# Pooled attention with a routed feed-forward network: row sums by a GpSimd add and block-wise VectorE sums, the ranking in smaller pieces, the first loads in halves

## The chip, the cores and the metric

The kernel runs on one core of one Trainium2 chip. The metric is device time in microseconds (us) of one execution. Three runs of the kernel before took 950.93, 951.79 and 951.79 us, median 951.79. A profiled execution took 951.33 us; its trace spans 949.5 us, and the remaining 1.8 us lie around the span. All numbers "from the trace" are of that execution.

A core has five engines that run side by side, each with its own queue, in order: TensorE (PE in the profile, with PEld for its weight loads), VectorE (DVE), ScalarE (ACT), GpSimd (POOL) and SyncE (SP), which here only issues transfers. An instruction at the head of a queue that waits for another engine holds up everything behind it in its own queue.

## The reference

```python
def _attn_ref(q, k, v):                      # B=8, H=8, S=1152, D=64, fp32
    q_pool = q.reshape(B, H, S // 2, 2, D).mean(axis=3)
    scores = np.matmul(q_pool, k.transpose(0, 1, 3, 2)) / np.sqrt(D)
    attn = np.exp(scores - np.max(scores, axis=-1, keepdims=True))
    attn = attn / (np.sum(attn, axis=-1, keepdims=True) + 1e-09)
    return np.matmul(attn, v)                # (8, 8, 576, 64)

def _moe_ref(x, w_gate, w1, w2, capacity):   # x (8, 576, 512), F=1024, capacity=128
    scores = np.einsum('bsd,d->bs', x, w_gate)
    out = x.copy()
    for b in range(B):
        top_idx = np.argpartition(-scores[b], capacity)[:capacity]
        xe = x[b, top_idx]
        ye = np.maximum(xe @ w1, 0.0) @ w2
        g = 1.0 / (1.0 + np.exp(-scores[b, top_idx]))
        out[b, top_idx] = x[b, top_idx] + g[:, None] * ye
    return out
```

Queries are pooled in twos, attention is computed for 64 heads, and the heads of a batch make a row of 512 per token. In each of the 8 batches the 128 tokens with the highest gate score go through a two-layer feed-forward network (FFN).

## The kernel before

**Pairs, halves, steps.** Two heads of a batch are a *pair* (32 pairs, 4 to a batch). A pair's 576 queries are two *halves* of 288 (s = 0, 1), and the 1152 keys of a half are taken in three *groups* (g = 0, 1, 2) of three 128-key chunks. One group of one half is a *step*. A pair has 6 steps, i = 0 to 5, the kernel 192, and `run` writes the work out step by step; nothing reorders it. In each step, `scores` (L710, L717) multiplies keys with queries, two heads beside each other in the array, and ScalarE takes the exponent into a tile `p` of 128 x 3 x 2 x 288; keys lie on partitions, so a row sum runs over partitions and chunks. `weighted` (L727) then multiplies the `p` of the step before with the values and accumulates `av` over the three groups. So TensorE's queue is: scores of this step, `av` of the last step, and what the step has besides.

**The row sums.** `added` adds the three `p` tiles of a half on VectorE: `acc` = p0 + p1 (L745, 1728 columns), `acc` += p2 (L745), then the three chunks of `acc` into `sum` (L755, L756, 576 columns each). In the first step of the next half, `drained` (L760) transposes `av` out of PSUM in 32 x 32 blocks into `avb`. In the second step of the next half, `normalized` lets TensorE sum `sum` over the partitions with a matrix of ones (L770, two products of 288 columns, one for each head); VectorE transposes the result out of PSUM (`smb`, L778), adds 1e-9, takes the reciprocal and multiplies `avb` with it into `x` (L786). After a pair's second half, `finished` (i = 1 of the next pair) stores `x` in DRAM by four transfers (`xs`, L798), multiplies it with the gate weights on GpSimd (`prod`, L803) and sums that on VectorE (`part`, L809).

**The FFN.** `routed` is a generator that `run` advances once in a step, but not in the steps that call `normalized`. It begins at i = 1 of the batch's following pair and does in turn: the gate scores of a batch into one row (`line`, `diag`, two products L842), the same as columns (`columns`, five small products), the rank of each of five token tiles (L880, L889, L899, two tiles between two yields), the choice of 128 tokens (`pick`, `rank`, products L926, `index`), the gather of their rows (L938, GpSimd's queue), its transposition (L953), two layers (L965 twice 32 product records, L977 16), and the scatter (L992). For the last batch all of it stands at the end, behind `outside`, which checks the row sums' bounds.

**Tiles that are reused.** All small products share the pool `ps_ms` with one PSUM buffer (`misc`), `av` has one (`ps_av`), the scores three (`ps_sc`), `p` has five SBUF buffers.

**Loads.** `load_pair` issues, all on SP, four quarters of keys (`kb`) and of queries (`qb`), 144 KB each in pieces of 128 bytes, and two transfers of values. `prepare_pair` pools the queries on GpSimd (`qp`, L692) and transposes keys and queries block-wise on VectorE (`kT` L697, `qT` L698). Pair n+1 is loaded at i = 0 of pair n and prepared at i = 3. SP runs ahead of the other engines: it is held by the four `xs` transfers, which wait for `x`, and by transfers under way, of which the program allows eight before it waits for the oldest. The FFN weights (4.2 MB) are loaded behind pair 1.

## Time and profile before

| what | value |
|---|---|
| median of three runs | 951.79 us |
| profiled execution, its span | 951.33 us, 949.5 us |
| busy: TensorE, VectorE, ScalarE, GpSimd | 844.1, 629.0, 359.5, 109.4 us |
| first scores start | 14.36 us |
| scores of pair 1 start | 34.23 us |
| last `av` starts, last instruction's issue starts | 892.5, 944.1 us |
| a batch in the steady state (588.9 to 702.1) | 113.2 us |
| granted TensorE clock, mean | 0.946 |

Busy time is summed over the whole span, and each engine's share is an average. A line of a group of instructions names the source line, the engine, the operation, output and input tiles and their shapes, the number of instructions, busy time and the mean duration of one. A line of waits says which engine's instruction sat idle for which other, how long in total, how often, and the longest. A line of the timeline has the start, the duration, the engine, the line, and in brackets the idle time before it and who ended it. A matrix product in fp32 shows as two records.

### The profile page before, as it was taken

The numbers are of one execution on the slowest core, as the hardware profiler recorded it, in microseconds if no ns is written. First come the engines' busy times: TensorE is split into PE (matmuls) and PEld (weight loads), VectorE is DVE, ScalarE is ACT, GpSimd is POOL, SyncE is SP. The second block draws the span as 40 slices with busy tenths as digits, with TensorE's granted clock in tenths as the row PEclk, the third lists the DMA queues.
The fourth block names the chain that finished last, engine by engine and source line by source line (L and its number), as shares of the span: only waits on it lengthen the run. The fifth ranks groups of instructions, "written<-read, shape, count | busy, mean of one in ns | idle before, by whom it ended". The sixth has DMA issues, their size and how long they took to land.

```text
span 949.5 us, 14253 instructions
## 1 busy us (share of the span) xinstructions
PE 844.1 (89%) x5695; PEld 500.2 (53%) x5695; DVE 629.0 (66%) x1069; ACT 359.5 (38%) x625; POOL 109.4 (12%) x91
## 2 busy tenths in 40 slices
PE   4999888998899988999879989799889998889736
PEld 2555545654456554565446545465455654556324
DVE  2888777566875678746787376865777567874540
ACT  2544443434343344325424344343443334433200
POOL 1111111011110111102011111011111011110100
PEclk9999998999999999999999999899998999989958
DMA  9987774766834676545767437557464667810120
GB/s 134 249 135 103 125 105 60 83 99 109 104 56 61 94 138 88 76 61 74 125 88 99 60 77 117 82 88 99 89 97 64 76 99 118 108 24 7 25 67 14
DMA packets 453419, 84.97 MB, mean 89 GB/s; under 512 B 450528, under 2 KB 450528, under 8 KB 453088
## 3 DMA queue, kind: packets, MB, share of 16 engines
q1 hardware_dynamic: 452064, 79.79, 57.5%
q0 software_dynamic: 1280, 4.20, 1.6%
q8 instruction: 46, 0.75, 0.4%
q14 instruction: 29, 0.24, 0.1%
HBM read 72.42 MB, written 20.97 MB: 98 GB/s over the span
## 4 chain that ended last, share of the span: by engine, by line
issue 39%; PE 27%; DVE 18%; SPq 5%; POOL 5%; DMA 4%; ACT 2%; POOLq 0%; DVEq 0%
PE sc L710 9%; PE av L727 8%; DVE acc L745 6%; PE ps L965 6%; DMA qb<-in_q_dram 3%; POOL qp L692 3%; SPq L675 2%; SPq L798 2%; DVE cmp L889 2%; PE ps L977 1%; SPq L678 1%; ACT p L717 1%; DVE sum L755 1%; POOL prod L803 1%; PE ps L926 1%
## 5 line engine op out<-in xcount | busy, mean ns | idle before, releaser
L717 ACT ACTIVATE p<-sc 128x576 f32<-128x576 f32 x576 | 336.1, 651 | 408.3 <-PE sc L710 389.6
L710 PE MATMUL sc<-qT,kT 64*128 64x288 f32 x2304 | 352.3, 438 | 9.9 <-DVE qT L698 9.9
L727 PE MATMUL av<-p,v_sb 128*64 128x288 f32 x2304 | 332.2, 425 | 22.7 <-DVE avb L760 22.7
L710 PEld LDWEIGHTS sc<-qT,kT 64*128 64x128 f32 x2304 | 221.0, 195 | 124.3 <-issue 71.8
L727 PEld LDWEIGHTS av<-p,v_sb 128*64 128x64 f32 x2304 | 152.3, 140 | 181.7 <-issue 77.1
L745 DVE TENSOR_TENSOR acc<-p 128x1728 f32<-128x1728 f32 x64 | 124.6, 1947 | 115.4 <-ACT p L717 115.1
L745 DVE TENSOR_TENSOR acc<-acc,p 128x1728 f32<-128x1728 f32 x64 | 137.0, 2141 | 10.0 <-ACT p L717 9.5
L803 POOL TENSOR_TENSOR prod<-x,w_gate 128x576 f32<-128x576 f32 x32 | 44.9, 1403 | 568.9 <-DVE x L786 568.9
L760 DVE STREAM_TRANSPOSE avb<-av 128x288 f32<-128x288 f32 x64 | 30.6, 478 | 60.0 <-PE av L727 60.0
L965 PE MATMUL ps<-xeT,w 128*128 128x128 f32 x512 | 63.4, 284 | 1.4 <-ACT hT L972 0.7
L965 PEld LDWEIGHTS ps<-xeT,w 128*128 128x128 f32 x512 | 60.3, 197 | 8.1 <-issue 5.3
L977 PE MATMUL ps<-w,hT 128*128 128x512 f32 x128 | 57.1, 599 | 0.7 <-ACT hT L972 0.7
L809 DVE TENSOR_REDUCE part<-prod 128x18 f32<-128x576 f32 x32 | 24.1, 753 | 48.7 <-POOL prod L803 48.7
L755 DVE TENSOR_TENSOR sum<-acc 128x576 f32<-128x576 f32 x64 | 49.6, 775 | 2.2
L756 DVE TENSOR_TENSOR sum<-sum,acc 128x576 f32<-128x576 f32 x64 | 49.6, 775 | 2.2
L692 POOL TENSOR_TENSOR qp<-qb 128x576 f32<-128x576 f32 x32 | 45.9, 1435 | 22.8 <-DMA qb<-in_q_dram 22.6
L697 DVE STREAM_TRANSPOSE kT<-kb 128x1152 f32<-128x1152 f32 x32 | 43.0, 1345 | 6.2 <-DMA kb<-in_k_dram 6.2
L770 PE MATMUL ps<-sum,ones 128*64 128x288 f32 x256 | 42.7, 413 | 1.5 <-DVE sum L756 1.5
L977 PEld LDWEIGHTS ps<-w,hT 128*128 128x128 f32 x128 | 23.7, 190 | 30.7 <-issue 29.8
L926 PE MATMUL ps<-meta,pick 128*128 128x3 f32 (+1 forms) x80 | 15.3, 310 | 27.3 <-DVE pick L916 27.3
L972 ACT ACTIVATE hT<-ps 128x512 f32<-128x512 f32 x16 | 9.6, 597 | 73.8 <-PE ps L965 73.8
L984 DVE SCALAR_TENSOR_TENSOR xe<-ps,own_gate,xe 128x512 f32<-128x512 f32 x8 | 6.0, 751 | 41.9 <-PE ps L977 41.9
(64 smaller groups left out, 307.6 us busy)
## 6 DMA issues: line engine op xcount, KB each, us to landing
kb<-in_k_dram SPq DMA_DIRECT2D x128, 144.0 KB, 4.6
qb<-in_q_dram SPq DMA_DIRECT2D x128, 144.0 KB, 4.8
v_sb<-in_v_dram SPq DMA_DIRECT2D x64, 288.0 KB, 5.3
xs<-x SPq DMA_DIRECT2D x128, 72.0 KB, 2.3
out_dram<-xs SPq DMA_DIRECT2D x8, 1152.0 KB, 5.7
w<-in_moe_w_dram SPq DMA_DIRECT2D x2, 2048.0 KB, 11.1
xe<-xs,index POOLq DMA_INDIRECT x8, 3.5
out_dram<-xe,index POOLq DMA_INDIRECT x8, 4.4
```

Source lines behind the costliest of these rows:

```text
L692: nc.gpsimd.tensor_tensor(out=qp[:, :, :], in0=pair["q"][:, :, 0, :], in1=pair["q"][:, :, 1, :], op=ALU.add)
L697: nc.vector.transpose(pair["kT"][:, :], pair["k"].rearrange("p n d -> p (n d)"))
L710: nc.tensor.matmul(sc[:, j, 0:n], lhsT=pair["kT"][rows, c * P : (c + 1) * P], rhs=pair["qT"][rows, qs], start=True, stop=True,)
L717: nc.scalar.activation(grp["p"][:, u, :, :], sc[:, :, 0:n], AF.Exp, scale=self.scale)
L727: nc.tensor.matmul(self.av[j * self.D : (j + 1) * self.D, 0:n], lhsT=grp["pair"]["v"][:, j, c, :], rhs=grp["p"][:, u, j, :], start=(c == 0 ...
L745: nc.vector.tensor_tensor(out=acc[:, :, :], in0=first[:, :, :], in1=grp["p"].rearrange("p u j n -> p u (j n)"), op=ALU.add,)
L755: nc.vector.tensor_tensor(out=to, in0=acc[:, 0, :], in1=acc[:, 1, :], op=ALU.add)
L756: nc.vector.tensor_tensor(out=to, in0=to, in1=acc[:, 2, :], op=ALU.add)
L770: nc.tensor.matmul(ps[j * self.D : (j + 1) * self.D, 0:n], lhsT=self.ones[:, 0 : self.D], rhs=half["sum"][:, j, :], start=True, stop=True,)
L803: nc.gpsimd.tensor_tensor(out=prod[:, :, :], in0=x[:, hp, :, :], in1=self.w_gate[:, hp : hp + 1, :].broadcast_to([P, self.QB, BLK]), op=AL ...
L965: nc.tensor.matmul(pv[:, f, 0:w], lhsT=self.w1[:, c, (f0 + f) * P : (f0 + f + 1) * P], rhs=xeT[:, c, 0:w], start=(c == 0), stop=(c == self ...
L977: nc.tensor.matmul(ps[0:w, 0 : self.Dm], lhsT=hT[:, f, 0:w], rhs=self.w2[:, f, :], start=(f == 0), stop=(f == self.NFC - 1),)
```

## The change

1. **Row sums.** `added` makes p0 + p1 on GpSimd in one add of 128 x 1728; p2 is left as it is. The new `folded`, called in the first step of the next half right after `drained`, sums both tiles on VectorE with a reduce over 32 columns that transposes each 32 x 32 block first (128 x 1728 in, 54 columns out), and a small reduce of the 108 results gives `sum`, now 128 x 18. `normalized` multiplies this with a constant 128 x 128 matrix `merge` in one product of 18 columns, which leaves each total where `avb` needs it; two additions of 1e-9 on 64 partitions each read PSUM directly, and `smb` is gone.
2. **The FFN's pieces.** The ranking yields after each tile; there is one yield more behind `pick`; and `routed` is advanced in every step, also in those that call `normalized`.
3. **Loads.** Pair 0 is loaded and prepared in two parts, its queries on ScalarE's queue, its keys and values on SP. Loads of a following pair, and the weights, are issued at i = 1; the weights now stand ahead of pair 1.
4. **The end.** After the last step, `misc` takes tiles of the scores' pool (three buffers), and `outside` is called behind the last gather's issue.

```diff
-    def load_pair(self, b, hp):
+    def load_pair(self, b, hp, parts=1):
...
+        nk, nq = self.KB // parts, self.QB // parts
+        other = nc.sync if parts == 1 else nc.scalar
+        for i in range(parts):
+            for j, ds, rows in self.quarters():
+                h = 2 * hp + j
+                nc.sync.dma_start(
+                    kb[rows, i * nk : (i + 1) * nk, :],
...
+                other.dma_start(
+                    qb[rows, i * nq : (i + 1) * nq, :, :].rearrange("i n r d -> i (n r) d"),
...
-    def prepare_pair(self, pair):
+    def prepare_pair(self, pair, parts=1):
...
+        for i in range(parts):
+            ks, qs = slice(i * nk, (i + 1) * nk), slice(i * nq, (i + 1) * nq)
+            nc.gpsimd.tensor_tensor(
+                out=qp[:, qs, :], in0=pair["q"][:, qs, 0, :], in1=pair["q"][:, qs, 1, :], op=ALU.add
+            )
...
     def added(self, grp, half):
...
         if grp["g"] == 1:
-            half["acc"] = self.work.tile([P, G, 2 * n], F32, name="acc")
...
+            half["fold"] = self.small.tile([P, 2, G * nb], F32, name="fold")
+            acc = self.work.tile([P, G, 2, n], F32, name="acc")
+            nc.gpsimd.tensor_tensor(
+                out=acc.rearrange("p u j n -> p (u j n)"),
+                in0=half["p0"].rearrange("p u j n -> p (u j n)"),
+                in1=grp["p"].rearrange("p u j n -> p (u j n)"),
+                op=ALU.add,
+            )
+            half["acc"] = acc
             return
-        half["sum"] = self.work.tile([P, 2, n], F32, name="sum")
-        to = half["sum"].rearrange("p j n -> p (j n)")
-        nc.vector.tensor_tensor(out=to, in0=acc[:, 0, :], in1=acc[:, 1, :], op=ALU.add)
-        nc.vector.tensor_tensor(out=to, in0=to, in1=acc[:, 2, :], op=ALU.add)
+        half["last"] = grp["p"]
+
+    def folded(self, half):
+        nc, nb = self.nc, 2 * self.HB
+        fold = half["fold"]
+        for a, of in enumerate((half["acc"], half["last"])):
+            nc.vector.tensor_reduce(
+                fold[:, a, :],
+                of.rearrange("p u j (m d) -> p (u j m) d", d=BLK),
+                AX.X,
+                ALU.add,
+                apply_transpose=True,
+            )
+        half["sum"] = self.small.tile([P, nb], F32, name="sum")
+        nc.vector.tensor_reduce(
+            half["sum"][:, :],
+            fold.rearrange("p a (u n) -> p n (a u)", n=nb),
+            AX.X,
+            ALU.add,
+        )
...
     def normalized(self, half):
-        ps = self.ps_ms.tile([P, 512], F32, name="ps")
+        ps = self.misc()
+        nc.tensor.matmul(
+            ps[:, 0 : 2 * hb],
+            lhsT=self.merge.rearrange("p g j -> p (g j)"),
+            rhs=half["sum"][:, :],
+            start=True,
+            stop=True,
+        )
+        tot = self.sums[:, half["at"], :]
         for j in range(2):
-            nc.tensor.matmul(
-                ps[j * self.D : (j + 1) * self.D, 0:n],
-                lhsT=self.ones[:, 0 : self.D],
-                rhs=half["sum"][:, j, :],
...
-        nc.vector.transpose(smb.rearrange("p n d -> p (n d)"), ps[:, 0:n])
...
+            rows = slice(j * self.D, (j + 1) * self.D)
+            nc.vector.tensor_scalar(
+                out=tot[rows, :],
+                in0=ps[rows, j * hb : (j + 1) * hb],
...
     def misc(self):
+        if self.ending:
+            return self.ps_sc.tile([P, 2, 512], F32, name="sc")[:, 0, :]
         return self.ps_ms.tile([P, 512], F32, name="ps")
...
-            if t % 2 == 1:
-                yield
+            yield
         nc.vector.tensor_reduce(rank[:, :], parts[:, :, :], AX.X, ALU.add)
...
+            if self.ending:
+                self.count = self.outside()
...
     def run(self):
-        upcoming = self.load_pair(*pairs[0])
-        self.prepare_pair(upcoming)
+        upcoming = self.load_pair(*pairs[0], parts=2)
+        self.prepare_pair(upcoming, parts=2)
...
+                if i == 1:
                     if n == 0:
                         self.load_weights()
+                    if following:
+                        upcoming = self.load_pair(*following)
...
             if step >= 1 and step % self.NG == 0:
-                self.drained(halves[step // self.NG - 1])
+                half = halves[step // self.NG - 1]
+                self.drained(half)
+                self.folded(half)
...
-            else:
-                next(routing, None)
-            if step < n_groups and i == 3 and n + 1 < len(pairs):
+            if step < n_groups and i == 3 and following:
                 self.prepare_pair(upcoming)
-        count = self.outside()
+            next(routing, None)
+        self.ending = True
```

## The prediction

> **What bounds the kernel now.** I read the busy times first, then TensorE's waits, then the timeline of a half without FFN work, then the granted clock in the gaps. TensorE is the bound, and its gaps are few:

> ```profile
> PE 844.1 (89%) x5695; PEld 500.2 (53%) x5695; DVE 629.0 (66%) x1069; ACT 359.5 (38%) x625; POOL 109.4 (12%) x91
> ...
> PE ps L926 <- DVE pick L916: 27.3, 8, 7.4
> PE av L727 <- DVE avb L760: 22.7, 10, 2.9
> PE ps L842 <- DVE diag L830: 19.6, 7, 2.8
> ```

> All three waits are for VectorE, two of them for ranking work queued ahead (`pick`, and an `avb` behind four tiles of ranking). Between them TensorE never waits:

> ```profile
> 669.33 1.73 PE L710 MATMUL sc<-qT,kT 64*128 64x288 f32 x12
> 669.44 0.48 DVE L760 STREAM_TRANSPOSE avb<-av 128x288 f32<-128x288 f32 x1 [0.53 <-PE av L727]
> 670.13 1.74 ACT L717 ACTIVATE p<-sc 128x576 f32<-128x576 f32 x3 [1.47 <-PE sc L710]
> 670.98 1.17 PEld L727 LDWEIGHTS av<-p,v_sb 128*64 128x64 f32 x12 [0.39 <-issue]
> ...
> 672.49 0.66 PE L770 MATMUL ps<-sum,ones 128*64 128x288 f32 x4
> 673.07 1.73 PE L710 MATMUL sc<-qT,kT 64*128 64x288 f32 x12
> ```

> A plain step takes 3.26 us (666.07 to 669.33), one with the totals' product 3.74, so a half 10.27. `sum` was ready (668.92) before this half's `av` ended at 669.33. To be seen: from that end the old chain has only `avb` left, and `avb` starts 0.11 later.

> A gap also costs clock. The columns here are time, then busy time by engine, then PEclk:

> ```profile
> 596.00:597.70 1.70, 0.00 (x0) 0.00 (x0) 1.70 (x10) 0.00 (x0) 0.00 (x0) 1.00 1.29 158
> 597.80:600.80 3.00, 3.00 (x14) 1.60 (x16) 3.00 (x13) 0.00 (x0) 0.00 (x0) 0.53 1.43 148
> ```

> After this gap of 2.92 us the next 3 us run at half clock. Of 14 gaps of 2.8 to 2.9 us, 10 are followed by that, at about 1.5 us each; all seven `pick` gaps (2.0 to 3.7 us) are; none of 0.57, 0.57 and 1.13 us is.

> **What goes.** (a) The product of 0.49 us becomes one of 18 columns. L965's records (weights and moving both 128 wide) take 0.118 us, `columns`' single records 0.07; two of between: 0.22. 64 x 0.27 = 17.3 us. (b) The two ranking waits, in 7 batches (the eighth's FFN is the tail): `avb` 7 x 2.92 = 20.4, slow clock 6.3 behind four of them; `pick` 19.9 idle and 17.4 slow (three times 3.4, four times 1.8, from L926's start to the next L770 against 1.0 + 3.17). Together 64.0. With one tile a step (1.2 us on VectorE) nothing of it is queued ahead of `avb`, and `pick` has two steps. (c) Three small `avb` waits of batch 0: 2.3. Sum -83.6.

> **What comes: the sums stand behind `av`.** VectorE's queue is now `avb`, block sum, block sum, small sum, and only then may TensorE's product run, which stands at the end of the next step. Count from the end of `av`: `avb` at 0.11; the next instruction 0.40 after it (50.09 to 50.49), at 0.51. A block sum reads 1728 columns: the straight reduce L809 takes 0.753 us for 576, L826 0.266 for 72, so 0.97 ns a column and 1.87 for 1728; L745 takes 1.96 for 1728 and transposes 1.35 for 1152 (1.06 ns a column, 1.95). I take 1.95, the transpose's line; the two follow each other at 1.87. Second ends at 0.51 + 1.87 + 1.95 = 4.33; small sum 0.04 later, 108 columns, 0.30: 4.67; hand-over 0.05: 4.72. TensorE is there at 3.26. It waits 1.46 us, and everything behind it, scores included, waits too. The bounds: no trace row has a reduce that transposes. Below, nothing excludes less than a straight reduce; from 1.22 each the wait is gone. Above, a transpose and then a reduce, 3.9 each, would make the wait 5.4.

> How often: batch 0 8 halves, the others 5 of 8 whole (FFN products cover the rest): 43 x 1.46 = 62.8. At pair 0, i = 4, behind L842's 0.69 it waits 0.77; at pair 2, i = 1, behind L926 (1.0) and held until `index` and `own_gate` have left the one PSUM buffer (4.95), 0.74: 7 x 1.51 = 10.6. Behind L965 (3.77) nothing.

> **The one PSUM buffer.** Routing now runs at i = 4 too. There `columns` needs the buffer that VectorE reads the totals from, and VectorE has `kT` and `qT` queued ahead of that read (1.26 + 0.66 after 4.62, then 0.25): 6.84 after `av`, TensorE there at 4.94. 1.9 x 7 = 13.3. It makes one gap of 2.9 us with the product between; taking 10 in 14 at 1.5, clock 7.5. L965's second block waits 0.35 the same way, L953 for the later gather 0.3: 4.6.

> **GpSimd's add.** 3 x 1.40 (L803, 576 columns) = 4.2 us, 3.8 if a part of a row is fixed. It starts when p1 is done: the second step's scores begin at 3.26 and its exponents end 2.54 later (669.33 to 671.87), so at 5.85 into a half with the hand-over; it ends at 10.05, and its block sum comes at about 15: covered by 4.7 us; if not, its whole lateness would land on the same wait. It sits ahead of `prod` and `qp` in GpSimd's queue. And it holds VectorE off:

> ```profile
> 24.10 2.40 POOL L692 TENSOR_TENSOR qp<-qb 128x576 f32<-128x576 f32 x1 [10.61 <-DMA qb<-in_q_dram]
> ...
> 25.27 1.85 DVE L755 TENSOR_TENSOR sum<-acc 128x576 f32<-128x576 f32 x1
> ...
> 27.15 0.76 DVE L756 TENSOR_TENSOR sum<-sum,acc 128x576 f32<-128x576 f32 x1
> ```

> The first add takes 1.85 instead of 0.76 while the other runs, and that takes 2.40 instead of 1.40 behind `acc`: they alternate. So `x`, two tiles in, waits until 10.05 instead of starting at 8.9 (the totals' product ends at 8.20, 0.7 for L780 to L784 as now); `prod`, `part`, `line`, `diag` follow (1.45, 0.79, 0.28, 0.79) and L842 starts at 13.9. TensorE is there at 11.5: 2.4, against 2.81 now; -2.8. This wait stays, clock loss and all. [...] If the second block sum did hold GpSimd, `x` would be 1.8 us later and the L842 waits 12 us longer in all.

> [...]

> **Loads.** First scores are now at 14.36. With halves, half the bytes land by about 6.5 (all eight by 11.9 now), scores can start near 8, but values are issued only when second halves have landed (about 10.5; now 7.95) and `av` starts near 17 or 18 instead of 19.10: -1. Then pair 1 stands behind the weights:

> ```profile
> 25.70 2.12 SPq L664 DMA_DIRECT2D w<-in_moe_w_dram  x1
> ...
> 43.25 1.92 SPq L678 DMA_DIRECT2D qb<-in_q_dram  x1
> ```

> Here the pair behind the weights (pair 2, not urgent) has its last queries 22.3 us after w2's issue (43.25 + 4.71). In the new order w2 is issued at about 16.2 (values 10.5 to 12.9, `w_gate` 2.88, w1), pair 1's queries land at 38.5, pooling and transposition take 2.2, its scores start at 40.7 instead of 34.23. +6, between -3 (weights go faster alone) and +9. ScalarE's eight issues end before its first scores. Later pairs are loaded a pair ahead: nothing.

> **The end.** `outside` (2.4 us, 901.56 to 903.98) goes under the gather, PSUM buffers save 1.1, the block sums cost 2.5 behind the last `av` (`x` 3.65 after `av` now, about 6.1 then): -1.

> **Sum.** -83.6 + 62.8 + 10.6 + 13.3 + 7.5 + 4.6 - 2.8 + 6 - 1 = +17.4. On the profiled execution's 951.3 (0.5 below the median): 969.

> **Rivals.** *Faster.* The block sums are shorter than a straight pass. It decides at 43 x 0.41 us: 1.75 a sum and less; from 1.22 the 62.8 and most of the 10.6 go, `columns` waits 0.6 instead of 1.9: 969 - 62.8 - 9 - 9 - 7 = about 881. [...] With part of that, or -3 at the start and no clock loss, 930 to 949. *Clock.* The 43 waits, 1.46 and a product that hardly loads the array, lie between 1.13 (never slow) and 2.0 (always): if half of them cost 1.5 us, +32, 1001; all, 1033. *Two passes.* Sums of 3.9: 57 waits of 3.9 more, 1190. *It does not do what it says:* GpSimd late by more than 4.7 us; 1.2 us a half for every 1.2 beyond, about 1030 at 6.

> **How the numbers follow.** A measurement tells from no change what is over 0.2% (1.9 us). Chances: slower near 969 (955 to 990) 0.53; clock 0.12; two passes or late GpSimd 0.05; faster 0.27, of which 0.10 near 881; within 0.2% 0.03. The range leaves out 881 and the two-pass case and half of the clock's: 928 to 1015. For the likeliest case alone 955 to 990.

> **What would show it.** Right: a wait of the 18-column product for the small sum, about 1.5 us, in some 40 places; `pick` and `avb` gone from TensorE's waits, `diag` still there at 2.4; a wait of `columns` for the totals' read; `x` held until the GpSimd add ends; a block sum near 1.95 us; pair 1's scores near 40. Wrong: block sums well under 1.75; slow clock behind the short waits; pair 1 in time.

## The result, and the profile after

The changed kernel takes 976.01 us (974.53 to 977.27) against 951.79: 1.0252 times the time before, 95% interval 1.0229 to 1.0276. Forecast was 969, slower. Its profiled execution takes 974.76 us with a span of 973.0, so 23.4 more than the profiled execution before; this is the difference that has to be accounted for.

The busy times of the kernel after, then TensorE's waits in it (total us, times, longest):

```profile
PE 825.7 (85%) x5567; PEld 493.2 (51%) x5567; DVE 578.7 (59%) x1008; ACT 358.4 (37%) x625; POOL 354.1 (36%) x156
```

```profile
PE ps L810 <- DVE sum L792: 74.1, 50, 4.8
PE ps L888 <- DVE diag L876: 14.1, 7, 2.0
PE ps L657 <- DVE sums L820: 12.7, 7, 1.8
PE sc L735 <- DVE qT L720: 12.2, 2, 8.1
```

TensorE works 18 us less than before and VectorE 50 us less, and the kernel is still slower. The `pick` and `avb` waits inside the loop are gone. One wait above all has taken their place: the 18-column product waits for `sum` 50 times (below, the norm wait), 49 of them in the loop. A half without FFN work, from the timeline:

```profile
668.16 1.73 PE L735 MATMUL sc<-qT,kT 64*128 64x288 f32 x12
668.28 0.48 DVE L801 STREAM_TRANSPOSE avb<-av 128x288 f32<-128x288 f32 x1 [2.52 <-PE av L752]
668.69 1.94 DVE L784 TRANSPOSE_TENSOR_REDUCE fold<-acc 128x54 f32<-128x1728 f32 x1
...
670.55 1.94 DVE L784 TRANSPOSE_TENSOR_REDUCE fold<-p 128x54 f32<-128x1728 f32 x1
670.86 3.83 POOL L770 TENSOR_TENSOR acc<-p 128x1728 f32<-128x1728 f32 x1 [3.78 <-ACT p L742]
672.52 0.34 DVE L792 TENSOR_REDUCE sum<-fold 128x18 f32<-128x108 f32 x1
...
672.91 0.40 PE L810 MATMUL ps<-sum,merge 128*128 128x18 f32 x2 [1.41 <-DVE sum L792]
...
673.24 1.73 PE L735 MATMUL sc<-qT,kT 64*128 64x288 f32 x12
...
673.97 1.04 DVE L830 TENSOR_TENSOR x<-avb,rec 128x288 f32<-128x288 f32 x1
```

The preceding `av` ends at 668.16. The product starts 4.75 us later (672.91), and VectorE is the reason, line by line: `avb`, two block sums, the small sum. TensorE was free 1.41 us earlier. The step takes 5.08 us; before it took 3.74.

### The profile page after: what moved, and what is told of

The parts are those of the page before. It is cut to its first block, busy times and chain, and to the rows that moved or that the text cites. A ratio compares the mean times of both kernels' runs of the same rounds, so it can differ in the third digit from the quotient of the medians.

```text
span 973.0 us, 14126 instructions
## 1 busy us (share of the span) xinstructions
PE 825.7 (85%) x5567; PEld 493.2 (51%) x5567; DVE 578.7 (59%) x1008; ACT 358.4 (37%) x625; POOL 354.1 (36%) x156
## 4 chain that ended last, share of the span: by engine, by line
PE 47%; DVE 23%; issue 14%; POOL 6%; DMA 5%; SPq 5%; POOLq 0%; ACT 0%; DVEq 0%
PE sc L735 16%; PE av L752 15%; DVE fold L784 14%; PE ps L1013 5%; PE ps L1025 5%; POOL acc L770 4%; DMA qb<-in_q_dram 3%; DVE avb L801 2%; PE ps L810 2%; SPq L686 2%; POOL prod L847 1%; SPq L692 1%; DVE sum L792 1%; DMA xs<-x 1%; DVE kT L716 1%
## 5 line engine op out<-in xcount | busy, mean ns | idle before, releaser
L770 POOL TENSOR_TENSOR acc<-p 128x1728 f32<-128x1728 f32 x64 | 245.9, 3842 | 356.7 <-ACT p L742 210.0
L784 DVE TRANSPOSE_TENSOR_REDUCE fold<-p 128x54 f32<-128x1728 f32 x64 | 123.9, 1935 | 0.0
L784 DVE TRANSPOSE_TENSOR_REDUCE fold<-acc 128x54 f32<-128x1728 f32 x64 | 123.8, 1935 | 0.0
L810 PE MATMUL ps<-sum,merge 128*128 128x18 f32 x128 | 25.4, 275 | 77.1 <-DVE sum L792 74.1
L830 DVE TENSOR_TENSOR x<-avb,rec 128x288 f32<-128x288 f32 x64 | 83.1, 1299 | 2.2
L810 PEld LDWEIGHTS ps<-sum,merge 128*128 128x128 f32 x128 | 19.4, 191 | 108.7 <-DVE sum L792 84.9
L1013 PE MATMUL ps<-xeT,w 128*128 128x128 f32 x448 | 53.5, 278 | 3.7 <-DVE sums L820 3.7
L1013 PEld LDWEIGHTS ps<-xeT,w 128*128 128x128 f32 x448 | 51.1, 192 | 7.3 <-PE ps L810 4.2
L713 POOL TENSOR_TENSOR qp<-qb 128x576 f32<-128x576 f32 (+1 forms) x33 | 45.0, 1363 | 25.3 <-DMA qb<-in_q_dram 25.3
L716 DVE STREAM_TRANSPOSE kT<-kb 128x1152 f32<-128x1152 f32 (+1 forms) x33 | 44.0, 1333 | 13.8 <-DMA kb<-in_k_dram 13.8
## 6 DMA issues: line engine op xcount, KB each, us to landing
w<-in_moe_w_dram SPq DMA_DIRECT2D x2, 2048.0 KB, 11.5
```

The costliest lines, as they stand in the source:

```text
L716: nc.vector.transpose(pair["kT"][:, i * nk * BLK : (i + 1) * nk * BLK], pair["k"][:, ks, :].rearrange("p n d -> p (n d)"),)
L770: nc.gpsimd.tensor_tensor(out=acc.rearrange("p u j n -> p (u j n)"), in0=half["p0"].rearrange("p u j n -> p (u j n)"), in1=grp["p"].rearra ...
L784: nc.vector.tensor_reduce(fold[:, a, :], of.rearrange("p u j (m d) -> p (u j m) d", d=BLK), AX.X, ALU.add, apply_transpose=True,)
L810: nc.tensor.matmul(ps[:, 0 : 2 * hb], lhsT=self.merge.rearrange("p g j -> p (g j)"), rhs=half["sum"][:, :], start=True, stop=True,)
L830: nc.vector.tensor_tensor(out=x[:, pair["hp"], s * hb : (s + 1) * hb, :], in0=half["avb"][:, :, :], in1=rec[:, :].unsqueeze(2).broadcast_t ...
L1013: nc.tensor.matmul(pv[:, f, 0:w], lhsT=self.w1[:, c, (f0 + f) * P : (f0 + f + 1) * P], rhs=xeT[:, c, 0:w], start=(c == 0), stop=(c == self ...
```

## The experiments

The prediction's theory: the waits above set the time, because the block sums stand behind `avb` in VectorE's queue. A first rival: work moved to GpSimd and VectorE costs by itself, and the waits only show where. A second question is whether the parts of the change add up, as the forecast's sum supposes. Slow clock means a granted TensorE clock (PEclk) of 0.5, half of the full one: in the kernel after, the scores of a step take 3.25 us at 0.50 (from 38.51) and 1.73 us at 1.00 (from 668.16).

**The third exponents' block sum ahead of `avb`.** Only its place in the queue changes; `fold_one` issues one block sum, of `acc` for 0 and of the third exponents for 1.

```diff
     def folded(self, half):
...
-        for a, of in enumerate((half["acc"], half["last"])):
-            nc.vector.tensor_reduce(
...
+        self.fold_one(half, 0)
...
+                self.fold_one(half, 1)
                 self.drained(half)
                 self.folded(half)
```

> The changed kernel, with one instruction earlier in VectorE's queue: the block sum over the third exponents stands ahead of avb. Nothing else is changed. Theory (the chain behind the end of av sets the time): after that end come avb (0.11 to 0.59), one block sum (to 2.45), the small sum (to 2.80) and the hand-over, so the 18-column product can run at 2.85 and TensorE, there at 3.26, no longer waits. Of the changed kernel's 976.0 go the 69.3 us of its waits inside the loop. Given back: TensorE now reaches the gate's product (L888) 1.4 us earlier while x is still held by the GpSimd add, 7 x 1.4 = 9.8, and perhaps slow clock behind those gaps (up to 7 x 1.5); the columns wait shrinks by 0.35 x 7. About 917 us, between 911 and 925, so below the kernel before (951.8). Rival (the work given to GpSimd and VectorE costs by itself, the waits only show where): the waits move to other places and no more than 20 us go, 955 or more.

Measured: 933.4 us, ratio to the kernel before 0.9808 (0.9774 to 0.9842). Moving one instruction is worth 42.6 us, more than the whole loss of 24.2; the first rival's "no more than 20" falls. It was right in part: 16 us of the forecast did not come, because waits came up in other places. TensorE's waits in this kernel:

```profile
PE ps L890 <- DVE diag L878: 24.5, 7, 3.5
PE av L752 <- DVE avb L803: 20.4, 7, 2.9
...
PE ps L812 <- DVE sum L794: 8.0, 14, 2.9
```

The norm wait has fallen from 74.1 to 8.0 and the `diag` wait has grown as expected, but an `avb` wait of 2.9 us in each of seven batches was not. Its start, in the timeline of one batch:

```profile
582.77 3.85 POOL L770 TENSOR_TENSOR acc<-p 128x1728 f32<-128x1728 f32 x1 [7.71 <-issue]
...
583.65 3.12 DVE L947 SCALAR_TENSOR_TENSOR tie<-sc_row,gate_sc,before 128x128 f32<-128x128 f32 x1
...
586.70 0.34 DVE L822 TENSOR_SCALAR sums<-ps 64x9 f32<-64x9 f32 x2
```

`tie` has two inputs, takes 0.35 us elsewhere, and here ends only when GpSimd's add does (586.77 and 586.62). The totals, `x`, `part`, two ranking tiles, a block sum and `avb` all come behind it.

**The add left out.** The same kernel without GpSimd's add; it leaves the second exponents out of the row sums:

```diff
-            nc.gpsimd.tensor_tensor(
-                out=acc.rearrange("p u j n -> p (u j n)"),
...
-            half["acc"] = acc
+            half["acc"] = half["p0"]
```

> The reordered kernel (third exponents' block sum ahead of avb) without GpSimd's add: the first block sum reads the first exponents alone, so the second exponents are left out of the row sums and the outputs are scaled wrongly. Theory (the add holds VectorE's two-input operations): x takes 0.46 us instead of up to 2.5, tie 0.35 instead of up to 3.1; the diag wait shrinks from 3.5 to 1.45 and loses its slow clock (7 x 2.06 + 15.6 = 30), the avb wait of 2.9 goes with its slow clock (27): 933.4 - 57 = 876, between 866 and 890. Rival (the add is hidden; these waits come from the order in VectorE's queue): 925 to 935, x and tie short but the waits as before.

Measured: 874.6 us, 0.9195 (0.9165 to 0.9225), 58.8 less. The groups of `x` and `tie` (count | busy us, mean ns), first with the add, then without:

```profile
L832 DVE TENSOR_TENSOR x<-avb,rec 128x288 f32<-128x288 f32 x64 | 115.3, 1801 | 2.2
L947 DVE SCALAR_TENSOR_TENSOR tie<-sc_row,gate_sc,before 128x128 f32<-128x128 f32 x32 | 30.5, 954 | 0.0
```

```profile
L825 DVE TENSOR_TENSOR x<-avb,rec 128x288 f32<-128x288 f32 x64 | 29.3, 458 | 2.2
L940 DVE SCALAR_TENSOR_TENSOR tie<-sc_row,gate_sc,before 128x128 f32<-128x128 f32 x32 | 11.1, 347 | 0.0
```

The add costs 59 us once the chain behind `av` is short. With it gone, the `diag` wait falls from 24.5 to 10.2 us, the `avb` wait from 20.4 to nothing, and the mean granted clock rises from 0.950 to 0.977. That GpSimd's own queue is to blame, where `prod` stands behind the add, can be ruled out at these two waits: in the kernel with the add, the add ahead of one `diag` wait ends at 557.06, `x` at 557.37, and `prod` starts at 557.45; ahead of the `avb` wait it ends at 586.62, and `prod` starts at 587.86. So the price is paid here by `x` and `tie` on VectorE, each of which reads two tiles or more: 115.3 us instead of 29.3 and 30.5 instead of 11.1 in all.

**One part alone.** The kernel before with the new row sums only, and with the FFN's pieces only:

> The kernel before with the new row sums alone; loads, ranking and end as before. Theory: 951.8, less 64 x 0.16 for the shorter product (0.33 instead of 0.49) and 2.3 for three avb waits of batch 0, plus norm waits of 1.41 in 43 halves and partly covered ones of 9: 951.8 - 10.2 - 2.3 + 60.6 + 9 = 1009; more where the ranking tiles now stand ahead of the block sums as well. 1000 to 1025. Rival (the row sums are about neutral and the loss comes from the spread of the FFN, by the one PSUM buffer): 940 to 965.

> The kernel before with only the FFN's pieces changed: one ranking tile a step, two steps for pick, a piece of FFN in the steps that normalize too. Theory: 951.8 - 64.0 (avb and pick waits with their slow clock) + 13.3 (columns behind the read of the totals) + 7.5 (clock behind it) + 4.6 (two small PSUM waits) = 913, between 903 and 925. Rival (ranking waits only move to the one PSUM buffer): 935 to 952.

Measured: row sums alone 958.1 us, 1.0074 (1.005 to 1.0098), some 50 less than forecast. Ranking alone 919.2 us, 0.9679 (0.9637 to 0.972), a time inside the forecast range. The waits of the kernel with the row sums alone explain the miss:

```profile
PE ps L810 <- DVE sum L792: 68.6, 43, 4.8
...
PE ps L810 <- DVE gate_sc L662: 9.3, 7, 1.3
PE ps L972 <- DVE pick L962: 7.4, 1, 7.4
PE av L752 <- DVE avb L801: 5.2, 4, 1.7
```

The norm waits are there about as computed (73.1 us in the loop with those behind `gate_sc`, against 69.6), but the seven `pick` waits of the loop (19.9 us), most of the 22.7 us of `avb` and all of the 19.6 us of `diag` are gone, although the ranking is still two tiles a step; the one `pick` wait that is left is the tail's. The old row sums held VectorE for 5.4 us of adds in each half, ahead of `avb`. Without them, two ranking tiles fit in most batches.

With the ranking alone the waits are these:

```profile
PE av L727 <- DVE avb L760: 21.3, 15, 2.4
PE ps L842 <- DVE diag L830: 16.7, 7, 2.4
```

The `pick` waits are gone here too, but the `avb` wait that the forecast struck out is nearly whole (22.7 us before), now without slow clock behind it (each `av` behind the seven waits of 2.39 us takes its plain 1.68): slow clock in the loop falls from 68 us to 14. The products on the one PSUM buffer wait 8.1 and 8.1 us, and no `columns` wait is followed by slow clock. So the forecast time was met by errors that cancel. What the two parts share is the `pick` waits and much of the slow clock: each removes them alone, and together they remove them once.

**The ranking undone in the changed kernel.** This puts the question directly.

```diff
-            yield
+            if t % 2 == 1:
+                yield
...
             yield
-            yield
             ps = self.misc()
...
+            else:
+                next(routing, None)
...
-            next(routing, None)
```

> The changed kernel with the FFN's pieces as before (two ranking tiles a step, one step for pick, no piece in the steps that normalize); row sums, loads and end as changed. Theory (the gains overlap: the row sums alone free VectorE enough for avb and pick, so the spread of the ranking brings nothing here and only costs the columns waits): 958.1 of the run with the row sums alone, plus 6 for the start (pair 1's first scores 4.3 later, 2.1 at half clock), less 2 for the end: 962, between 957 and 967; faster than the changed kernel. Rival (the parts add, as the prediction counted them: 64.0 saved by the spread against 25.4 of columns and PSUM waits): 976 + 38.6 = 1015; with the 32.5 measured for the ranking alone, 1008.

Measured: 957.65 us, 1.0071 (1.0041 to 1.0101), 18.4 faster than the changed kernel; the rival needs 1008 or more. The same edit that is worth -32.5 us alone costs +18.4 on top of the row sums. Two of this run's waits, which lists none for `diag`:

```profile
PE ps L810 <- DVE gate_sc L662: 9.3, 7, 1.3
PE sc L735 <- ACT p L742: 3.7, 7, 0.5
```

The theory blamed the `columns` waits, but their 12.7 us in the changed kernel only replace these 13.0. What the spread adds there is the `diag` wait (14.1 us, as the gate's product now comes a step earlier), 5.5 of norm waits and 3.7 at L1013.

**The old order of the loads**, halves kept, in the changed kernel and on top of the ranking alone:

```diff
-                if i == 1:
-                    if n == 0:
-                        self.load_weights()
-                    if following:
-                        upcoming = self.load_pair(*following)
+                    if following:
+                        upcoming = self.load_pair(*following)
+                    if n == 0:
+                        self.load_weights()
```

> The changed kernel with the old order of the loads: pair 1 is loaded at the first step, ahead of the weights; the first pair still comes in halves on two queues. Theory: the wait for qT at 38.5 (8.1 us) and the half clock behind it (2.0 to 2.4) go, all else as in the changed kernel: 966, between 963 and 969. Rival (pair 1 ahead of the weights takes bandwidth from the first pair's values, or w_gate then comes late): 971 to 977.

> The kernel before with the spread of the FFN's pieces and the first pair in halves on two queues, pair 1 still ahead of the weights, old row sums and old end. Theory: 919.2 of the run with the spread alone, less 5.8 (first scores at 8.6 instead of 14.4): 913, between 909 and 917. Rival (the early start is lost again at the first values or at pair 1): 917 to 921.

Measured: 964.6 us in the changed kernel, 1.0125 (1.0077 to 1.0173), 11.4 less than with the weights ahead of pair 1, though its eight runs spread from 954.7 (clock 0.974) to 968.7 (0.959); here is the wait that went, and the slow steps behind it (a plain one has 1.73 and 1.68), in the kernel after:

```profile
38.51 3.25 PE L735 MATMUL sc<-qT,kT 64*128 64x288 f32 x12 [8.08 <-DVE qT L720]
41.70 2.27 PE L752 MATMUL av<-p,v_sb 128*64 128x288 f32 x12
```

On the ranking alone, halves bring nothing: 919.0 us against 919.2, the rival's case. The first `av` starts 5.3 us earlier (13.66 against 18.92), but pair 2 then makes TensorE wait 1.41 us at 51.37, an `avb` behind it costs 1.95 at 58.31, and the first `diag` product starts only 1.6 us earlier.

**Placing the pieces.** If the loss is one of place, other steps for the FFN's pieces should recover it. To the reordered kernel with the old load order, this gives one tile in every third step (but the first two are neighbours), and moves the gate's products and `columns` away from the totals' product. Not shown below: one `yield` fewer behind `pick`, one more behind the gather and behind `xeT`.

```diff
         yield
+        yield
         sc_row = ffn.tile([P, Sp], F32, name="sc_row")
...
             nc.scalar.copy(sc_row[:, cols], ps[:, 0 : self.HALF])
             yield
+            if s == 0:
+                yield
...
-            yield
+            for _ in range((1, 3, 3, 3, 0)[t]):
+                yield
```

> The changed kernel with the third exponents' block sum ahead of avb, the old order of the loads, and the FFN's pieces put in other steps: the gate's two products two and four steps after diag (now one and two), columns at a step without a totals' product, one ranking tile in every third step (after x, so after the GpSimd add), the gather's product in the step after pick. Theory (the remaining waits are a matter of place): 933.4 of the reordered run, less 11.4 (loads), 24.5 and 15.6 (diag waits and the slow clock behind them), 20.4 and 6.6 (avb waits and clock), 5.7 (columns), 8.0 (norm waits), plus some 6 for the one pair of tiles in neighbouring steps and PSUM waits: 847, between 838 and 870. Rival (VectorE, 67% busy with pieces of 2 us and held by the GpSimd add, has no slack where it counts; waits come up elsewhere): 890 to 922.

Measured: 893.6 us, 0.9378 (0.9341 to 0.9415), 47 short of the forecast and inside the rival's band. One `avb` wait of 3.55 us in each of seven batches was left, each followed by slow clock (the `av` behind it takes 2.93 to 3.15 us instead of 1.68). In that half `part` waited 5.33 us for `prod`, which stood behind the add in GpSimd's queue, and two tiles and a block sum stood behind `part`. The next run moves `part`, whose reduce is now in `parted`:

```diff
-        nc.vector.tensor_reduce(half["part"][:, hp, :], prod[:, :, :], AX.X, ALU.add)
+        half["prod"] = prod
+        if hp == self.NPAIR - 1:
+            self.parted(half)
...
             next(routing, None)
+            if step >= self.NG + 2 and step % self.NG == 2:
+                half = halves[step // self.NG - 1]
+                if half["s"] == 1 and half["pair"]["hp"] < self.NPAIR - 1:
+                    self.parted(half)
```

> The run with the placed pieces, with one more instruction moved: for all but the last pair of a batch, part's reduce stands in VectorE's queue one step later, behind the ranking tile. There it waited for prod, which stands behind the 3.85 us GpSimd add in GpSimd's queue, and held two ranking tiles, the block sum and avb behind it. Theory: the seven avb waits of 3.55 us (24.9) and the slow clock behind them (14.4) go: 893.6 - 39 = 855, between 848 and 864. Rival (VectorE has no slack for two tiles in one half, so tie or avb is late all the same): 875 or more.

Measured: 862.8 us, 0.906 (0.9041 to 0.9079), the best version here. Its waits:

```profile
PE ps L812 <- DVE sum L794: 12.9, 25, 0.6
PE av L752 <- DVE avb L803: 10.1, 8, 1.4
```

The wait is down to 1.35 us and has no slow clock behind it (1.68 us for the `av` in all seven batches). Ahead of what is left of it, the first of the two tiles is held by the add again; that this is the cause was not tested by a run of its own.

```profile
641.73 3.85 POOL L770 TENSOR_TENSOR acc<-p 128x1728 f32<-128x1728 f32 x1 [9.48 <-issue]
...
642.45 3.28 DVE L956 SCALAR_TENSOR_TENSOR tie<-sc_row,gate_sc,before 128x128 f32<-128x128 f32 x1
```

**The same places with the old row sums**, to see what the new ones are worth:

> The kernel before, old row sums, loads and end, with the FFN's pieces in the same steps as in the run with the placed pieces. It measures what placing alone is worth, and so what the new row sums bring when both are placed. Theory (the loss of the changed kernel is one of place, and the row sums themselves bring little: 64 x 0.16 for the product, 3 for the loads and the end): 919.2 of the spread ranking, less 21.3 (avb), 16.7 and some 6 (diag and clock), 16.2 (columns and hidden-layer PSUM waits) and plus 5: 864, between 853 and 885. Rival (VectorE's adds on the way to avb leave no room: the avb waits stay): 895 to 920, so that the new row sums are worth 30 us or more.

Measured: 917.1 us, 0.9641 (0.9612 to 0.9669): the rival's case. Waits for `avb` total 30.8 us, with the adds directly ahead of it in the queue. The new row sums with their order mended, together with the halves, the end and `part` moved, are worth 54 us; put where the change put them, they cost.

## Why the prediction was right, and where its sum was not

The direction and the mechanism held: the sums behind `av` set the step. Term by term, in the profiled executions (predicted, then measured):

| term | predicted us | measured us |
|---|---|---|
| totals' product | -17.3 | -10.2 (slot 0.33, not 0.22: 64 x 0.16) |
| ranking waits and slow clock, batch 0 | -66.3 | both waits (42.6) gone from the loop; the whole taken as predicted |
| norm waits | 62.8 + 10.6 | 72.3 (74.1 less 4.8 in the tail, plus 3.0 behind `own_gate`) |
| `columns`, waits and clock | 13.3 + 7.5 | 12.7 and about 12 (one norm wait's 1.4 included) |
| other PSUM waits | 4.6 | 3.7 |
| `diag` wait | -2.8 | -5.5, and about -4 of slow clock |
| loads | 6 - 1 | 6.4 (pair 1 at 38.51, 4.3 later; 2.1 at half clock) |
| end | -1 | -2.3 (51.5 us from the end of the last `av` to the span's end, before 53.8) |

The right column adds up to about 19 of the 23.4; the rest I cannot place.

## What to carry to other kernels

When a sum of gains and losses is made part by part, ask of each gain whether another part already brings it: two edits that free the same engine can remove the same wait, and it goes once, while each keeps its own cost. Work that the bounding engine waits for should not stand in a helper's queue behind the result that starts the chain, if it can be done earlier; a block sum placed before `avb` instead of after it was worth 43 us. An add that seemed hidden on GpSimd was paid for by `x` and `tie` on VectorE (1.80 us in the mean instead of 0.46, and 0.95 instead of 0.35) and, in the placed kernel, by `prod` behind it in GpSimd's own queue; so place those, and whatever queues behind them, after it or out of its way.

## What was not expected

The product of 18 columns, two records, holds TensorE for 0.33 us until the next scores start; two records of L965 in the kernel before, with 128 columns each, take 0.24 in a row of such. A `tie` of 0.35 us became 3.12 and 3.28 while a 128 x 1728 GpSimd add ran. And VectorE's share did not tell how much room it had: it is busy 59% of the changed kernel, which waits 74.1 us for its sums, and 72% of the best version, which lets TensorE work 93% of the span.
